# DMA loads tied to TensorE's progress, x tiles first, other DMA constants in the planner's model, and attention-weight normalisation in four parts, in a one-core kernel for linear attention and a gated MLP

## The chip, the cores and the metric

The kernel runs on one core of a Trainium2 chip. The metric is the device time of one execution, in microseconds (us). Lower is better. A profile shows a single execution; its span is some 1.8 us shorter than the device time of the same execution, and executions of one kernel on one chip differ, so times are compared by runs and gaps by profiles.

## The reference

Layernorm of x, then two branches on it: a linear-attention branch (32 heads of 32) and a gated MLP. The output is x + s * silu(mlp).

```python
x = A_x                                   # [1, 2048, 1024] bf16
xn = layernorm(x)
qkv = xn @ wqkv                           # heads: 32 of 32
pq, pk = phi(q), phi(k)                   # phi(t) = (t+1 if t>0 else exp(t)) + 1e-6
kv  = pk^T v ; z = sum_s pk               # per head
s   = ((pq kv) / (pq z + 1e-6)) @ wo
b   = (silu(xn @ w_gate) * (xn @ w_up)) @ w_down      # hidden size 3584
out = x + s * silu(b)
```

## The kernel before

The kernel is not written engine by engine. It calls helpers that record operations (engine, what is read and written, a planned duration). A *planner* then runs a small model of the engines over the recorded operations and fixes the static order of the instructions on TensorE (PE), VectorE (DVE), ScalarE (ACT), GpSimd and the DMA queue of SyncE (SP). Each engine executes its list in that order, waiting on semaphores. So the planner's durations decide no wait, but they decide what stands *behind* a wait.

```python
class Plan:
    def schedule(self):
        for o in reversed(ops):                       # latest start, from TensorE's cumulated work
            d = o.pecum if o.eng == "pe" else o.pecum + 30.0
            for s in o.succs:
                extra = (2.5 + o.nbytes / 250e3) if o.sem is not None else o.busy + o.lat
                d = min(d, s.dl - extra)
            o.dl = d - o.urgent
        # ... list scheduling: each engine takes, of what is ready, the earliest deadline;
        # ... TensorE takes the first ready of the next 6 operations in program order
            if o.sem is not None:                     # a DMA: one queue, in order
                free[e] = s + 0.08
                b = max(s + 0.7, dma_free)
                dma_free = b + o.nbytes / 300e3
                o.done = dma_free + 1.4
```

A DMA with no operand to wait for goes out as soon as its buffer is free. The attention weights are normalised in one piece per half of the rows (`p`): the reciprocals of the denominators are stored to DRAM, and 16 broadcasts bring them back; ACT scales each tile and DVE multiplies.

```python
def x_load(i):
    s = x_ring.take()                                 # 4 slots
    dma([], [s.r], s.ap(), xf[i*128:(i+1)*128, :], dsem(...), 256 * KB)

def normalise(p):                                     # called once per p, after weight pair 1
    for j in range(2):
        for hl in range(4):
            for q in range(2):
                dma([rscr], [rbr], rb[32*hl:32*hl+32, :, q, :], rows[:, q, :].partition_broadcast(32), ...)
        for g in range(8):
            act([z_r, zrr], [zrr], zr, zr, ACT.Identity, "sb", scale=zc[:, g:g + 1])
            tt([sr, zrr], [sr], dst, src, zr, ALU.mult, True)
    # ... four stores of 512 KB to q_scratch, read back for the last stage

def m_load(c):                                        # last stage: one buffer (MR) for four blocks c
    raw = W.at(MR, 4 * KB, FP16)...
    dma([mscr], [rr], raw, m_v[:, :, c*256:(c+1)*256], dsem("mld"), 512 * KB)
```

Order of the work: layernorm, transposes and k, v for 16 tiles (to 136 us); q, gate and up in weight pairs, first half of the rows (to 367); down-projection and combined attention weights `m` in four column blocks (to 467); the same two stages for the second half.

## Time and profile before

Three runs: 786.19, 787.03 and 787.52 us, median 787.03.

The busy line of the page, and the first line of the chain of work that ended last. In all profile lines PEld is TensorE's load of weights, SPq the sequencer of the DMA queue, `L195` a line of kernel.py; "..." marks lines left out.

```profile
PE 763.0 (97%) x3818; PEld 347.7 (44%) x3818; DVE 513.2 (65%) x945; ACT 305.0 (39%) x507; POOL 11.5 (1%) x33
...
PE 81%; DMA 10%; ACT 4%; DVE 3%; SPq 2%; issue 1%; ACTq 0%
```

TensorE is busy 763 of 787.9 us. Its 128x512 products last 379 ns each and start every 216 ns in a steady stretch. The Trainium skill ("TensorE: Matmul & The Clock Gate", Single matmul latency and Back-to-back issue gap) gives the formulas for these two numbers, (398 + N)/2.4 and N/2.4 + 2.5 ns, and the trace agrees with both. The page gives the second for an isolated product and about 131 ns for a real stream of weight loads and products at N = 512; this trace, which is such a stream, shows 216. A consequence for reading: an "idle before" of a product is what is left after the previous product's 379 ns, so the delay is about 0.16 us longer than that column says.

Since only TensorE's gaps can be won, they are read one by one. TensorE's timeline of before near the normalisation (start, length, what, in brackets the idle time before and who ended it):

```profile
196.75 17.44 PE L195 MATMUL ps<-X,W 128*128 128x512 f16 x80
215.74 3.63 PE L195 MATMUL ps<-X,W 128*128 128x512 f16 x16 [1.55 <-ACT ps L308]
219.96 6.28 PE L195 MATMUL ps<-X,W 128*128 128x512 f16 x28 [0.59 <-DVE ps L315]
227.25 13.12 PE L195 MATMUL ps<-X,W 128*128 128x512 f16 x60 [1.02 <-ACT ps L308]
```

That is 3.2 us of idle TensorE. The same view near 41 us, where a layernorm tile is late:

```profile
41.33 0.62 PE L202 MATMUL ps<-ident,W 128*128 128x128 f16 x8 [1.32 <-DVE veps L449]
...
43.07 1.90 PE L195 MATMUL ps<-H,X 128*128 128x512 bf16 x8 [0.65 <-ACT X L308]
```

And the DMA queue's timeline (start, time the queue's sequencer spent, what) for the time before that:

```profile
14.70 2.97 SPq L318 DMA_DIRECT2D W<-in_B_w_gate_dram  x1
17.71 1.72 SPq L318 DMA_DIRECT2D W<-in_B_w_up_dram  x1
19.47 4.78 SPq L318 DMA_DIRECT2D H<-in_A_wo_dram  x2
24.29 4.90 SPq L318 DMA_DIRECT2D W<-in_A_wqkv_dram  x2
29.23 30.57 SPq L318 DMA_DIRECT2D W<-in_A_x_dram  x10
```

x tile 4 is issued at 29.2, behind weights that are first needed after 136 us. In the last stage DVE is the one that stands. Its timeline, and then TensorE's:

```profile
382.96 0.69 DVE L315 TENSOR_TENSOR TM<-ps,TM 128x512 f32<-128x512 f32 x1 [1.67 <-PE ps L195]
391.31 2.98 DVE L315 TENSOR_TENSOR W<-W 128x896 f16<-128x896 bf16 x6 [7.67 <-DMA W<-in_B_w_down_dram]
394.21 0.69 DVE L315 TENSOR_TENSOR ps<-ps,TM 128x512 f32<-128x512 f32 x1
```

```profile
394.96 1.69 PE L195 MATMUL ps<-H,W 128*128 128x512 f16 x7 [1.25 <-DVE ps L315]
```

DVE waits 7.67 us for a down-projection weight block, then combines weights for 3 us, and only then does the addition in PSUM (394.21) that TensorE needs. Only two of the six combinations are of that block, from 391.31 to 392.6; the other four are of the `m` block, and wait for its reload. The chain that ended last runs through that reload (start, length, what):

```profile
386.19 6.53 DMA W<-m_scratch
392.74 1.11 DVE W L315 x3
...
394.21 0.70 DVE ps L315
```

Without these four the addition could have come some 1.6 us earlier (an estimate, 394.21 less 392.59), more than the gap of 1.25. The view of who waited for whom (total us, times, longest; in the same view ACT waits twice for broadcasts, at most 2.9 us):

```profile
DVE W L315 <- DMA W<-in_B_w_down_dram: 34.3, 8, 7.7
```

### The profile page before, as it was taken

The numbers are of one execution on the slowest core, as the hardware profiler recorded it, in microseconds if no ns is written. First come the engines' busy times: TensorE is split into PE (matmuls) and PEld (weight loads), VectorE is DVE, ScalarE is ACT, GpSimd is POOL, SyncE is SP. The second block draws the span as 40 slices with busy tenths as digits, with TensorE's granted clock in tenths as the row PEclk, the third lists the DMA queues.
The fourth block names the chain that finished last, engine by engine and source line by source line (L and its number), as shares of the span: only waits on it lengthen the run. The fifth ranks groups of instructions, "written<-read, shape, count | busy, mean of one in ns | idle before, by whom it ended". The sixth has DMA issues, their size and how long they took to land.

```text
span 787.9 us, 9684 instructions
## 1 busy us (share of the span) xinstructions
PE 763.0 (97%) x3818; PEld 347.7 (44%) x3818; DVE 513.2 (65%) x945; ACT 305.0 (39%) x507; POOL 11.5 (1%) x33
## 2 busy tenths in 40 slices
PE   8999999999999999999999999999999999999997
PEld 3445555444434444444444444344444444444443
DVE  5587432768597766886365676788776768557353
ACT  3344443555573334322222245547333332232131
POOL 2020000000000000000000000000000000000000
PEclk9999999999999999999999999999999999999999
DMA  9921000232883233370633623279423242251510
GB/s 310 277 67 41 1 1 1 81 107 63 190 246 106 73 89 106 94 222 9 197 92 82 183 71 96 66 156 296 143 63 106 76 126 62 59 171 50 154 41 27
DMA packets 142893, 86.74 MB, mean 110 GB/s; under 512 B 3328, under 2 KB 138752, under 8 KB 142848
## 3 DMA queue, kind: packets, MB, share of 16 engines
q1 hardware_dynamic: 142848, 86.13, 38.8%
q8 instruction: 30, 0.49, 0.3%
q14 instruction: 15, 0.12, 0.1%
HBM read 75.50 MB, written 10.62 MB: 109 GB/s over the span
## 4 chain that ended last, share of the span: by engine, by line
PE 81%; DMA 10%; ACT 4%; DVE 3%; SPq 2%; issue 1%; ACTq 0%
PE ps L195 79%; DMA W<-m_scratch 4%; ACT H L308 2%; PE ps L202 2%; SPq L318 2%; DMA H<-in_A_wqkv_dram 1%; DMA W<-in_B_w_down_dram 1%; DMA H<-r_scratch 1%; DVE W L315 1%; DMA W<-in_B_w_up_dram 1%; ACT TM L308 1%; DVE ps L315 1%; DMA m_scratch<-H 0%; DVE TM L315 0%; ACT ps L308 0%
## 5 line engine op out<-in xcount | busy, mean ns | idle before, releaser
L195 PE MATMUL ps<-X,W 128*128 128x512 f16 x1504 | 346.7, 379 | 7.7 <-DVE TM L315 2.8
L308 ACT ACTIVATE TM<-ps 128x512 f32<-128x512 f32 (+2 forms) x300 | 177.0, 596 | 302.6 <-PE ps L195 302.2
L195 PEld LDWEIGHTS ps<-X,W 128*128 128x128 f16 (+1 forms) x1504 | 143.4, 98 | 184.5 <-DVE ps L315 5.7
L315 DVE TENSOR_TENSOR W<-W 128x1024 f16<-128x1024 bf16 (+3 forms) x224 | 137.3, 629 | 73.2 <-DMA W<-in_B_w_down_dram 34.3
L195 PE MATMUL ps<-H,W 128*128 128x512 f16 x672 | 153.3, 379 | 4.2 <-DVE ps L315 4.0
L195 PE MATMUL ps<-P,W 128*128 128x512 f16 x512 | 122.9, 379 | 1.5 <-ACT ps L308 1.5
L195 PEld LDWEIGHTS ps<-H,W 128*128 128x128 f16 (+1 forms) x672 | 64.7, 98 | 82.2 <-DVE ps L315 7.1
L315 DVE TENSOR_TENSOR ps<-ps,TM 128x512 f32<-128x512 f32 x80 | 55.6, 695 | 69.5 <-PE ps L195 69.5
L315 DVE TENSOR_TENSOR TM<-ps,TM 128x512 f32<-128x512 f32 (+1 forms) x112 | 68.2, 610 | 36.5 <-PE ps L195 27.0
L308 ACT ACTIVATE ps<-ps 128x512 f32<-128x512 f32 x80 | 47.0, 587 | 101.2 <-PE ps L195 101.0
L195 PEld LDWEIGHTS ps<-P,W 128*128 128x128 f16 (+1 forms) x512 | 49.2, 98 | 60.8 <-ACT ps L308 2.0
L315 DVE TENSOR_TENSOR H<-ps,TM 128x512 f16<-128x512 f32 x84 | 57.4, 685 | 4.7 <-PE ps L195 3.3
L195 PE MATMUL ps<-H,X 128*128 128x512 bf16 x256 | 57.3, 379 | 2.6 <-ACT X L308 1.8
L195 PE MATMUL ps<-H,P 128*128 128x512 bf16 x256 | 56.6, 379 | 0.0
L308 ACT ACTIVATE TM<-TM 128x512 f16<-128x512 f32 (+1 forms) x54 | 33.5, 620 | 56.6 <-DVE TM L315 56.4
L315 DVE TENSOR_TENSOR H<-H 128x1024 f16<-128x1024 f16 (+1 forms) x74 | 41.6, 571 | 12.2 <-ACT H L308 11.2
L494 DVE TENSOR_SCALAR TM<-TM 128x512 f16<-128x512 f16 x64 | 17.9, 290 | 41.6 <-ACT TM L308 41.1
L195 PEld LDWEIGHTS ps<-H,X 128*128 128x128 f16 x256 | 24.4, 98 | 31.0 <-ACT X L308 2.1
L195 PEld LDWEIGHTS ps<-H,P 128*128 128x128 f16 x256 | 24.7, 98 | 28.3
L315 DVE TENSOR_TENSOR W<-H 128x1024 f16<-128x1024 f16 x38 | 25.4, 685 | 0.5
L308 ACT ACTIVATE H<-H,zc 128x512 bf16<-128x512 bf16 x32 | 20.8, 716 | 5.0 <-DMA H<-r_scratch 5.0
L495 DVE SCALAR_TENSOR_TENSOR W<-ps,TM 128x512 bf16<-128x512 f32 x32 | 22.0, 688 | 0.8
(60 smaller groups left out, 307.9 us busy)
## 6 DMA issues: line engine op xcount, KB each, us to landing
W<-in_B_w_gate_dram SPq DMA_DIRECT2D x28, 512.0 KB, 3.9
W<-in_B_w_up_dram SPq DMA_DIRECT2D x28, 512.0 KB, 5.2
W<-in_B_w_down_dram SPq DMA_DIRECT2D x16, 896.0 KB, 7.1
W<-in_A_x_dram SPq DMA_DIRECT2D x16, 256.0 KB, 4.1
H<-in_A_wqkv_dram SPq DMA_DIRECT2D x4, 1024.0 KB, 8.8
W<-in_A_wqkv_dram SPq DMA_DIRECT2D x8, 512.0 KB, 7.5
TM<-in_A_x_dram SPq DMA_DIRECT2D x16, 256.0 KB, 4.2
H<-r_scratch SPq DMA_DIRECT2D x32, 128.0 KB, 4.2
```

Source lines behind the costliest of these rows:

```text
L195: last = h.matmul(o, l, r, start=st, stop=sp, skip_group_check=True)
L202: last = h.transpose(o, i, ident)
L308: return PL.op("act", reads, writes, lambda h: h.activation(o, i, func, **kw), nel(o) / 1200.0 + (0.055 if src == "ps" else 0.095))
L315: return dve(reads, writes, lambda h: h.tensor_tensor(o, a, b, op), nel(o), 1.92 if fast else 0.96)
L318: return PL.op("sp", reads, writes, lambda h: h.dma_start(o, i), 0.08, sem=s, nbytes=nbytes, cow=cow)
L494: dve([e.r], [b.r], lambda h: h.tensor_scalar(ba, ea, 1.0, EPS_PHI, ALU.min, ALU.add), 512, 2.6)
L495: dve([src_r, b.r], [out_r], lambda h: h.scalar_tensor_tensor(out_ap, src, 0.0, ba, ALU.max, ALU.add), 512)
```

## The change

The intent: (1) every load gets an extra predecessor, the TensorE operation that the plan places 12 us before the load's latest start, so that loads stop running far ahead of need; x tiles get 10 us of priority; the deadline allowance of a DMA grows. (2) The planner's model of a DMA becomes slower. (3) The normalisation is cut into four parts, spread over weight pairs 2 and 3, its broadcasts held to a TensorE product.

```diff
-                extra = (2.5 + o.nbytes / 250e3) if o.sem is not None else o.busy + o.lat
+                extra = (4.0 + o.nbytes / 200e3) if o.sem is not None else o.busy + o.lat
...
+        pes = [o for o in ops if o.eng == "pe"]
+        cum = [o.pecum + o.busy for o in pes]
+        for o in ops:
+            if o.sem is not None and o.succs:
+                k = bisect_right(cum, o.dl - self.lead) - 1          # lead = 12.0
+                if k >= 0 and pes[k] not in o.preds:
+                    o.preds.add(pes[k])
+                    pes[k].succs.append(o)
...
-                b = max(s + 0.7, dma_free)
-                dma_free = b + o.nbytes / 300e3
-                o.done = dma_free + 1.4
+                b = max(s + 1.0, dma_free)
+                dma_free = b + o.nbytes / 230e3
+                o.done = dma_free + 1.8
...
-            dma([], [s.r], s.ap(), xf[i * 128:(i + 1) * 128, :], dsem("x%d" % s.k), 256 * KB)
+            dma([], [s.r], s.ap(), xf[i * 128:(i + 1) * 128, :], dsem("x%d" % s.k), 256 * KB).urgent = 10.0
...
-        def normalise(p):
-            for j in range(2):       # 8 broadcasts, then 8 scalings and products; twice
+        def normalise_part(p, j, half):   # 4 broadcasts (after=PL.lastpe), 4 scalings and products, 1 store
...
+                    if 2 <= n <= 3:
+                        at = tuple((4 + 6 * h, partial(normalise_part, p, n - 2, h)) for h in range(2))
-                    normalise(p)
```

The denominators' scratch also gets another layout, so that a broadcast reads runs of 1 KB in place of 512 bytes.

More of the change, by code (lines that the diff above doesn't have):

```diff
@@ L1 @@
+from bisect import bisect_right
 from collections import deque
@@ L35, with __init__ @@
     LAT = {"pe": 0.22, "act": 0.2, "dve": 0.2, "pool": 0.2}
-    def __init__(self, window):
+    def __init__(self, window, lead):
         self.ops = []
@@ L42, in __init__, with op @@
         self.window = window
-    def op(self, eng, reads, writes, fn, busy, sem=None, nbytes=0, urgent=0.0, cow=None):
+        self.lead = lead
+    def op(self, eng, reads, writes, fn, busy, sem=None, nbytes=0, urgent=0.0, cow=None, after=None):
         o = Op()
@@ L55, in op @@
             preds.update(cow.preds)
+        if after is not None:
+            preds.add(after)
         for r in writes:
@@ L77, in op @@
             self.pecum += busy
+            self.lastpe = o
         self.ops.append(o)
@@ L203, in _tr_group, with build_kernel @@
     return last
-def build_kernel(nc, A_x, A_wqkv, A_wo, B_w_gate, B_w_up, B_w_down, out, WINDOW=6, NWARM=14):
+def build_kernel(nc, A_x, A_wqkv, A_wo, B_w_gate, B_w_up, B_w_down, out, WINDOW=6, NWARM=14, LEAD=12.0):
     S, D, FF = 2048, 1024, 3584
@@ L264, in build_kernel @@
         q_scr = nc.dram_tensor("q_scratch", [2, 2, 2, 128, 4 * 512], FP16)
-        r_scr = nc.dram_tensor("r_scratch", [2, 4, 32, 256], BF16)
+        r_scr = nc.dram_tensor("r_scratch", [2, 2, 32, 512], BF16)
         ps = [es.enter_context(nc.psum_tensor("ps%d" % b, [128, 512], F32)) for b in range(8)]
@@ L287, in dsem @@
             return semn[name]
-        PL = Plan(WINDOW)
+        PL = Plan(WINDOW, LEAD)
         MM = 0.2137
@@ L315, in tt, with dma @@
             return dve(reads, writes, lambda h: h.tensor_tensor(o, a, b, op), nel(o), 1.92 if fast else 0.96)
-        def dma(reads, writes, o, i, s, nbytes, cow=None):
-            return PL.op("sp", reads, writes, lambda h: h.dma_start(o, i), 0.08, sem=s, nbytes=nbytes, cow=cow)
+        def dma(reads, writes, o, i, s, nbytes, cow=None, after=None):
+            return PL.op("sp", reads, writes, lambda h: h.dma_start(o, i), 0.08, sem=s, nbytes=nbytes, cow=cow,
+                         after=after)
         class Ring:
@@ L774, in recip @@
             act([rr], [er], rb, ra, ACT.Identity, "sb")
-            dma([er], [named("rscr", p)], r_scr[p].rearrange("q h t -> (q h) t"), rb, dsem("rs"), 64 * KB)
-        RB0 = 68 * KB
-        def normalise(p):
-            for j in range(2):
-                rb = H.at(RB0 + j * 8 * KB, 8 * KB).rearrange("p (g q t) -> p g q t", g=NG, q=2)
-                rbr = H.reg(RB0 + j * 8 * KB, 8 * KB)
-                first = None
-                for hl in range(4):
-                    rows = r_scr[p, 2 * j:2 * j + 2, :, :].rearrange("q (g h) t -> h g q t", h=4)[hl]
-                    for q in range(2):
-                        o0 = dma([named("rscr", p)], [rbr], rb[32 * hl:32 * hl + 32, :, q, :],
-                                 rows[:, q, :].partition_broadcast(32), dsem("rr%d_%d_%d" % (j, hl, q)), 128 * KB, first)
-                        first = first or o0
-                for g in range(NG):
-                    src, sr = pq_tile(g, j)
-                    dst = src.bitcast(FP16)
-                    o = RB0 + j * 8 * KB + g * KB
-                    zr, zrr = H.at(o, KB), H.reg(o, KB)
-                    act([z_r, zrr], [zrr], zr, zr, ACT.Identity, "sb", scale=zc[:, g:g + 1])
-                    tt([sr, zrr], [sr], dst, src, zr, ALU.mult, True)
-            for j in range(2):
-                for k in range(2):
-                    o = PQ0 + (2 * k + j) * 4 * KB
-                    dma([H.reg(o, 4 * KB)], [named("q", p, k, j)], q_scr[p, k, j], H.at(o, 4 * KB, FP16),
-                        dsem("pq%d%d" % (k, j)), 512 * KB)
@@ new lines, in recip @@
+            o0 = None
+            for q in range(4):
+                t0 = (q % 2) * 256
+                o1 = dma([er], [named("rscr", p)], r_scr[p, q // 2, :, t0:t0 + 256], rb[32 * q:32 * q + 32, :],
+                         dsem("rs%d" % q), 16 * KB, o0)
+                o0 = o0 or o1
+        RB0 = 68 * KB
+        def normalise_part(p, j, half):
+            o = RB0 + (2 * j + half) * 4 * KB
+            rb, rbr = H.at(o, 4 * KB).rearrange("p (g t) -> p g t", t=512), H.reg(o, 4 * KB)
+            first = None
+            for hl in range(4):
+                rows = r_scr[p, j].rearrange("(g h) t -> h g t", h=4)[hl, 4 * half:4 * half + 4]
+                o0 = dma([named("rscr", p)], [rbr], rb[32 * hl:32 * hl + 32, :, :], rows.partition_broadcast(32),
+                         dsem("rr%d_%d_%d" % (j, half, hl)), 128 * KB, first, PL.lastpe)
+                first = first or o0
+            for gl in range(4):
+                g = 4 * half + gl
+                src, sr = pq_tile(g, j)
+                dst = src.bitcast(FP16)
+                zr, zrr = H.at(o + gl * KB, KB), H.reg(o + gl * KB, KB)
+                act([z_r, zrr], [zrr], zr, zr, ACT.Identity, "sb", scale=zc[:, g:g + 1])
+                tt([sr, zrr], [sr], dst, src, zr, ALU.mult, True)
+            o = PQ0 + (2 * half + j) * 4 * KB
+            dma([H.reg(o, 4 * KB)], [named("q", p, half, j)], q_scr[p, half, j], H.at(o, 4 * KB, FP16),
+                dsem("pq%d%d" % (half, j)), 512 * KB)
@@ L818, in gu_load, with gu_pair @@
             return wload([wg_v[:, :, n * 256:(n + 1) * 256], wu_v[:, :, n * 256:(n + 1) * 256]])
-        def gu_pair(p, n, stat):
+        def gu_pair(p, n, stat, at=()):
             sgs = {}
@@ L831, in ev_u @@
                 tt([r, s.r], [orr], o, ap, s.ap(FP16), ALU.mult)
-            run_pair(xset(stat, 0, XV[p], ev_g, d_ring), xset(stat, 1, XV[p], ev_u, d_ring))
+            run_pair(xset(stat, 0, XV[p], ev_g, d_ring), xset(stat, 1, XV[p], ev_u, d_ring), at)
             if n % 2 == 1:
@@ L1001, in build_kernel @@
                 else:
-                    gu_pair(p, n, st)
+                    at = ()
+                    if 2 <= n <= 3:
+                        at = tuple((4 + 6 * h, partial(normalise_part, p, n - 2, h)) for h in range(2))
+                    gu_pair(p, n, st, at)
                 pump(2)
```

## The prediction

> **What bounds it now.** TensorE. The page shows PE busy 763.0 of 787.9 us (97%), clock 1.00 in all stages. Steady matmuls follow each other every 0.215 us in the timeline; the change leaves their number alone. Only PE's idle time can be won: 24.9 us. Its parts in the PE timeline: start, 8.3-13.4: 1.9; 41.3-43.1: 2.0 (a layernorm tile); 140: 0.3; 174.9: 0.9; 215.7-227.3: 3.2 (ACT, DVE); 373-377: 1.1; 395: 1.3; 423: 0.3; 531.9: 1.5; 554.0: 1.1; 650.8: 1.7; 679: 1.4; 695-698: 0.8; 744: 1.2; end: 1.5.
>
> **What the change does, and the gap it meets.**
> 1. *x tiles first, weights held back.* The SP timeline shows x tile 4 issued only at 29.2, behind 5 MB of weights not needed before 136; it landed at 36.5. The Trainium skill ("DMA: Bandwidth & Descriptors", Queues, rings and completion order) says that each DMA engine consumes descriptors in ring order; this trace agrees: loads issued 10.7-29.2 landed in order of issue, 8.5-11 us later. With those held back, the 2.0 us at 41-43 goes. At the start two more x tiles come before the first weight load (about 0.85 us each at that window's 310 GB/s), but PE then has several tiles for each weight block: about 0, +1 at worst.
> 2. *Normalisation in quarters.* Now 16 broadcasts go out in one burst (0.45-0.5 us each on SP; landing 208.3-218.4), ACT sits in order behind them (2.9 us at 213.4), then mixes 16 scalings of 0.71 us with evictions PE waits for. Four parts, each with 4 broadcasts held to a PE product, half the descriptors, spread over two weight pairs: I expect 2.5 of 3.2 back near 215-227, 1.3 of 1.5 at 532, 1.0 of 1.1 at 554 (there the weight load took 8.7 us behind q stores and reloads; the reloads are now held back).
> 3. *A slower DMA in the planner's model* (230 GB/s, 1.8 us tail). It fixes the static order of DVE. Today DVE is ordered to combine a weight block that has not landed: it stood 7.7 us (382-391) and 2.3 (647-649.5) for down-projection weights, and PE's gaps at 395 and 650.8 follow. The old model gives a lone 896 KB load 5 us; the trace shows 5.9-9.8. The new one, 6.8 alone and 10.8 as second of a pair, fits. I expect 3.5 back of the 5.9 at 395, 423, 651, 679 and 744.
>
> Unchanged: 140, 175, 373 and 695 (one buffer for the combined weights), the end.
>
> **Added.** Only waits of the DMA queue. Each load still goes out some 18 us of PE work before its use, against 4-10 us to landing.
>
> **Sum.** 2.0 + 2.5 + 1.3 + 1.0 + 3.5 = 10.3 off; minus 1.8 for new short stalls, as every static order is redone: 8.5. **Predicted 778.5 us, 772.5 to 784.5.** Faster by over 2% (under 771.3) 0.07, within 2% 0.90, slower 0.03.
>
> **To see in the profile.** PE busy about 763, span near 779; no PE gap near 40; DMA rate low from 20 to 110 us, the first pairs' weights issued after 100; four groups of four broadcasts; no DVE wait above 3 us for down-projection weights; no weight load of 8 us near 545.
>
> **What would make it wrong.** Held loads bunching before the last stage (down weights, reloads, m) into a new DMA wait; ACT ordered to scale before a broadcast lands, in four places instead of one; a first weight block over 1 us later; DVE, 95% busy at 220-240, remaining the brake there.

## The result, and the profile after

Three runs: 774.91, 776.97 and 777.79 us, median 776.97, against 787.03 before. The ratio is 0.9868 (95% interval 0.9835 to 0.9902). Ratios here and below are the mean time of one kernel's runs over that of the other's runs of the same rounds, so they are not quite the ratio of the medians. In a later measurement of five rounds the changed kernel had a median of 776.51 us against 789.5, ratio 0.9849 (run e4 below). The two profiled executions, 789.71 (not one of the three runs above) and 774.91 us, happen to lie further apart than the medians.

The page of after:

```profile
PE 759.9 (98%) x3802; PEld 349.8 (45%) x3818; DVE 519.1 (67%) x945; ACT 306.2 (40%) x507; POOL 11.7 (2%) x33
...
PE 94%; ACT 2%; DVE 2%; DMA 1%; issue 0%; POOL 0%
```

The chain that ended last had 10% of its time on DMAs and now has 1%. (Of this trace 16 matmul records are missing; the work is the same.) TensorE's timeline near the normalisation is one unbroken row where before there were three gaps:

```profile
195.53 44.63 PE L209 MATMUL ps<-X,W 128*128 128x512 f16 x206
```

The DMA queue's timeline: x tiles no longer stand behind weights, and the first pairs' weights go out after 115 us.

```profile
10.22 79.12 SPq L332 DMA_DIRECT2D W<-in_A_x_dram  x12
115.94 1.00 SPq L332 DMA_DIRECT2D W<-in_A_wqkv_dram  x2
```

DVE's timeline in the last stage: the addition in PSUM at 387.08 now comes before the weight combination, and DVE's longest wait for that block is 1 us.

```profile
379.31 0.69 DVE L329 TENSOR_TENSOR TM<-ps,TM 128x512 f32<-128x512 f32 x1 [1.68 <-PE ps L209]
387.08 0.70 DVE L329 TENSOR_TENSOR ps<-ps,TM 128x512 f32<-128x512 f32 x1 [7.08 <-PE ps L209]
...
391.44 0.62 DVE L329 TENSOR_TENSOR W<-W 128x896 f16<-128x896 bf16 x1 [0.99 <-DMA W<-in_B_w_down_dram]
```

And the wait shown of before (ACT's longest wait for a broadcast is now 0.7 us):

```profile
DVE W L329 <- DMA W<-in_B_w_down_dram: 3.0, 3, 1.1
```

What got worse: the start. TensorE's idle before 15 us grew from 1.9 to 2.8 us in this profile (4.1 in that of e4). Layernorm of tile 1 is mixed into that of tile 0 here, and the transposes of tile 1 stand before the second product; but another order only moved the gaps (e10 below), so the cause is not shown.

### The profile page after: what moved, and what is told of

Its sections match the earlier page's. It is cut to its first block, busy times and chain, and to the rows that moved or that the text cites. A ratio compares the mean times of both kernels' runs of the same rounds, so it can differ in the third digit from the quotient of the medians. Undisturbed runs are those within 1.5% of the kernel's fastest.

```text
span 773.2 us, 9708 instructions
## 1 busy us (share of the span) xinstructions
PE 759.9 (98%) x3802; PEld 349.8 (45%) x3818; DVE 519.1 (67%) x945; ACT 306.2 (40%) x507; POOL 11.7 (2%) x33
## 4 chain that ended last, share of the span: by engine, by line
PE 94%; ACT 2%; DVE 2%; DMA 1%; issue 0%; POOL 0%
PE ps L209 92%; PE ps L216 2%; DMA W<-m_scratch 1%; ACT H L322 0%; DVE W L329 0%; ACT TM L322 0%; DMA W<-in_A_x_dram 0%; ACT L322 0%; DVE TM L329 0%; ACT X L322 0%; ACT ps L322 0%; DVE ps L329 0%; DVE stats L461 0%; DVE stats L462 0%; DVE H L600 0%
## 5 line engine op out<-in xcount | busy, mean ns | idle before, releaser
L329 DVE TENSOR_TENSOR W<-W 128x1024 f16<-128x1024 bf16 (+3 forms) x224 | 134.2, 628 | 10.8 <-PE ps L209 4.7
L209 PE MATMUL ps<-W 128*128 128x512 f16 x76 | 21.8, 379 | 0.0
```

The costliest lines, as they stand in the source:

```text
L209: last = h.matmul(o, l, r, start=st, stop=sp, skip_group_check=True)
L329: return dve(reads, writes, lambda h: h.tensor_tensor(o, a, b, op), nel(o), 1.92 if fast else 0.96)
```

## The experiments

The change has three parts that can be switched separately: **G** (gates, deadline allowance, x priority), **S** (the planner's DMA model) and **Q** (quarters). Theory M: S mends everything that depends on the static order, G only the late x tile, Q part of the normalisation. Rival G: the gates do it all, by keeping loads from crowding each other. Rival Q: quarters are what cures the normalisation. Twelve kernels ran; all gave correct results. Each was compared, in five rounds, with the kernel before on the same chip (its median there 788.7 to 789.6 us); e1 to e4, e5 to e8, e9 to e11 and e12 had a chip each, so runs of different groups are compared by their ratios. First the summary; the columns on the right are sums of TensorE's gaps of over 0.2 us in the profile of each run, by stretch (before: first profile and first measurement, while the ratios are to the kernel before on the run's own chip; the stretches move by a few us between kernels; "start" leaves out the first 1.4 us, and in before a gap of 0.15).

| run | parts | median us | ratio, 95% interval | start, to 30 | x tile, 41-45 | 214-230 | 365-377 | 393-425 | 530-555 | 640-682 | 683-698 | 705-745 |
|---|---|---|---|---|---|---|---|---|---|---|---|---|
| before | none | 787.0 | 1 | 1.8 | 2.0 | 3.2 | 1.1 | 1.5 | 2.6 | 3.1 | 0.6 | 1.2 |
| e1 | S | 779.38 | 0.9879 (0.9852-0.9907) | 3.3 | 2.9 | 0.8 | 0.6 | 0 | 0.8 | 0 | 1.1 | 0 |
| e2 | G | 784.30 | 0.9941 (0.9920-0.9962) | 4.6 | 0 | 2.7 | 1.3 | 0 | 2.5 | 0 | 0.7 | 0 |
| e3 | Q | 786.94 | 0.9975 (0.9949-1.0001) | 1.8 | 2.2 | 2.1 | 0.6 | 1.8 | 1.9 | 1.3 | 0.6 | 1.2 |
| e5 | S Q | 778.13 | 0.9849 (0.9826-0.9873) | 2.6 | 2.3 | 0 | 1.0 | 0 | 0 | 0 | 0.6 | 0 |
| e6 | G Q | 781.31 | 0.9891 (0.9870-0.9913) | 2.1 | 0 | 2.0 | 1.6 | 0 | 2.0 | 0 | 1.8 | 0.2 |
| e7 | G S | 784.24 | 0.9938 (0.9914-0.9962) | 2.3 | 0 | 2.4 | 1.8 | 0 | 2.9 | 0 | 0.7 | 0 |
| e4 | G S Q | 776.51 | 0.9849 (0.9823-0.9875) | 4.1 | 0 | 0 | 2.4 | 0 | 0 | 0 | 0.7 | 0 |

### e1, e2, e3: each part alone, and e4, all together

Edits: the kernel before with only the DMA model lines (e1), only the gate, allowance and priority lines (e2), only the quarters (e3); e4 is the changed kernel.

```diff
# e1, all that acts (the record's diff also carries unused parameters)
-                b = max(s + 0.7, dma_free)
-                dma_free = b + o.nbytes / 300e3
-                o.done = dma_free + 1.4
+                b = max(s + 1.0, dma_free)
+                dma_free = b + o.nbytes / 230e3
+                o.done = dma_free + 1.8
```

> The kernel before with one line group changed: the planner simulates a DMA as 1.0 us + bytes at 230 GB/s + 1.8 us (was 0.7, 300 GB/s, 1.4). No load is held, the normalisation is whole. Theory M (the model corrects the static order of DVE and ACT): the TensorE gaps of the last stages at 395, 423, 651, 679 and 744 (5.9 us together) mostly go, no DVE wait above 3 us for down-projection weights, the gap at 41-43 stays: about 782, 4 to 6 us faster. Rival G (the gates do it, by keeping loads from crowding each other): under 1.5 us faster, the gaps at 395 and 651 stay.

> The kernel before with the gates alone: every load held to a TensorE product, x tiles first, larger allowance in the deadlines; old DMA model, whole normalisation. Theory M: the gap at 41-43 (2.0 us) goes, perhaps that at 554 (1.1), up to 1 us is lost at the start; the gaps at 395, 651, 679, 744 and 215-227 stay: about 784.5, 1 to 4 us faster. Rival G: 6 us or more faster, with the gaps of the last stages gone.

> The kernel before with the normalisation in four parts alone (its broadcasts held to a TensorE product, nothing else held), old DMA model. Theory M: the gaps at 215-227 (3.2 us) and 532 (1.5) shrink to under 1.5 together, that at 41-43 and those of the last stages stay: about 783, 3 to 5 us faster. Rival G: with the old model and ungated loads the broadcasts still land late, ACT stands in four places: under 2 us faster.

> The changed kernel once more, on the same chip as the three parts: 775 to 778 if the first measurement holds. If the parts act on separate gaps, the three single gains add up to about this gain; if they need each other, their sum is clearly smaller.

Measured: 1.2% faster by the model alone, more than expected; 0.6% by the gates alone; 0.25% by the quarters alone, with an interval that touches no change (theory M had expected 3 to 5 us of them: a miss). The three gains add to 2.05% and the whole gave 1.51%, so they overlap. Three numbers in the planner gave most of the gain, and they also cleared most of the *normalisation's* gaps, which the prediction had put down to the quarters; what the numbers changed in the order there was not read. Rival G is half right: the gates alone also cleared 393-425, 640-682 and 705-745, as I had said they would not. With quarters alone, the normalisation's gaps only fell from 3.2 to 2.1 and from 2.6 to 1.9.

What was wrong with the old model is told by one comparison. The planner's own reckoning is a by-product of the program, so its time for each DMA can be set beside the time that the trace shows from issue to landing, and its length for the whole program beside the span. Means, in us:

```
                              down-projection block   m reload        whole program
                              planned   trace         planned trace   planned   span
before                        5.70      7.01          3.98    5.14    769.8     787.9
S alone (e1)                  7.99      6.88          6.39    4.60    784.9     776.6
after                         7.72      6.44          6.95    5.10    772.1     773.2
```

Before, the planner was optimistic by 1.2 to 1.3 us for these loads. It placed the combination of a block where it believed the block had landed, ahead of additions that TensorE waits for (six of them at 391.31 above). Its plan was 18 us shorter than the span. With a pessimistic model the plan is longer (in e1 by 15 us, of which a wait of 10.8 for the x tile near 54, where the trace of e1 shows 2.9) and the execution shorter. The DVE wait itself is not the harm. In e1 DVE still waits for these blocks, five times and up to 6.0 us, and the addition in PSUM is still ordered behind the wait, yet TensorE has no gap there. DVE's timeline of e1:

```profile
380.46 0.69 DVE L321 TENSOR_TENSOR TM<-ps,TM 128x512 f32<-128x512 f32 x1 [1.68 <-PE ps L201]
385.59 1.28 DVE L321 TENSOR_TENSOR W<-W 128x896 f16<-128x896 bf16 x2 [4.44 <-DMA W<-in_B_w_down_dram]
389.74 0.70 DVE L321 TENSOR_TENSOR ps<-ps,TM 128x512 f32<-128x512 f32 x1 [2.86 <-PE ps L201]
```

Two combinations stand before the addition in place of six (those of the `m` block now come after it, from 390.9 on), and it is the addition that waits, 2.86 us, for TensorE. The block also lands earlier, 5.1 us after the start of the operation at 380.46, against 8.3 us after the same operation at 382.96 in before: the model sets the order of the DMA queue too, and in e1 one load of x goes out ahead of the block, in before two. Which of the two changes of order did more was not tested.

The x tile is another matter. It is late because weights are in front of it, and the new constants leave them there; e1's TensorE timeline keeps the gap:

```profile
42.71 0.62 PE L208 MATMUL ps<-ident,W 128*128 128x128 f16 x8 [2.04 <-DVE veps L456]
...
44.67 1.67 PE L201 MATMUL ps<-H,X 128*128 128x512 bf16 x7 [0.87 <-ACT X L314]
```

### e5, e6, e7: all but one part, and e8, all but the x priority

Edits: the changed kernel without the gates, allowance and priority (e5), with the old DMA model (e6), with `normalise` whole (e7), without `.urgent = 10.0` (e8).

> DMA model and quarters, no load held, x tiles not first. The model alone left gaps of 2.9 us near 42-45 (x tile), 0.8 near 225 and 0.8 near 539. Theory M (the model mends all that depends on static order, the gates only the x tile): the gap near 42 stays at 2 to 3 us, those at 225 and 539 shrink, last stages clean: ratio to before about 0.987, some 2 us slower than the whole change. Rival G: the last stages get gaps back, ratio above 0.991.

> Gates, x tiles first and quarters, with the old DMA model in the planner. Gates alone had already cleared the gaps at 395, 651 and 744, but not those near 219-227 (2.7) and 536-544 (2.5). Theory M: those near 215-230 and 535-545 stay at over 1.5 us each, quarters or not, since ACT is still ordered too early; ratio 0.990 to 0.995. Rival Q (quarters cure the normalisation once loads are held): both stretches under 0.5 us, ratio 0.985 to 0.987 like the whole change.

> Gates, x tiles first and the DMA model, with the normalisation whole. Theory M: the model alone had brought the normalisation's gaps from 3.2 to 0.8 and from 1.5 to 0.8, so at most 1.5 us slower than the whole change: ratio 0.985 to 0.987. Rival Q: gaps of 2 us or more return at 215-227, ratio 0.989 or above.

> The whole change without the 10 us of priority for x tiles. If x tiles first costs time at the start (two x tiles ahead of the first weight block, and layernorm of tile 1 mixed in before tile 0 is done), TensorE's gaps before 15 us shrink from 2.8-4.1 to about 1.8 and nothing comes back at 41-43, because holding the weights is what lets x tile 4 through: 1 to 2 us faster than the whole change, ratio about 0.983. If the priority is what lets the x tiles through, a gap of 2 us returns near 41-43 and the ratio rises to 0.988.

Measured: e5 0.9849, as fast as the whole within the intervals, where theory M had expected some 2 us slower; the gap near 42 stays, as it said, but the start is shorter (2.6 us, against 4.1 in e4). So once the model and the quarters are in, the gates, with the priority and the allowance, add nothing that these runs can resolve. e6 0.9891: the normalisation's stretches keep 2.0 us each, quarters or not, as theory M said. e7 0.9938: a miss for theory M, as rival Q had it. Gates and model together, with the burst, are slower than the model without gates (0.9879). e8 0.9839 (0.9815 to 0.9862, median 777.19), again not distinguishable from the whole. The x tiles get through without priority (no gap near 42), so holding the weights is what lets them through; but the start did not get shorter: gaps of 1.12 at 8.8 and 2.89 at 15.3 and two small ones, 4.5 us in all. So the priority is worth nothing that these runs can resolve.

In e7 a gap also slows what follows it. TensorE's timeline, and then the windows view (stretch, length, busy time and count of PE, PEld, DVE, ACT and POOL, granted clock, DMA share, GB/s):

```profile
229.06 7.30 PE L209 MATMUL ps<-X,W 128*128 128x512 f16 x26 [2.35 <-DVE ps L329]
```

```profile
226.00:229.00 3.00, 0.71 (x4) 0.10 (x2) 2.62 (x7) 3.00 (x7) 0.00 (x0) 0.96 0.94 281
229.00:232.00 3.00, 2.94 (x7) 1.04 (x8) 2.81 (x6) 0.58 (x2) 0.00 (x0) 0.50 1.18 325
232.00:236.00 4.00, 4.00 (x20) 1.83 (x19) 2.90 (x6) 1.71 (x3) 0.00 (x0) 0.98 0.29 115
```

After the gap the granted clock is 0.50: 7 products in 3 us, where 4 us at nearly the full clock hold 20. The clock record of this trace gives 3.41 us at 0.5 from 228.8. TensorE worked in the last 3.1 us of them; half of that, 1.5 us, is an estimate of the extra loss. The same happened once in e3 (from 215.4, after a gap of 2.13) and in e5 (from 42.8, after 2.04). The Trainium skill ("TensorE: Matmul & The Clock Gate", Part 1) says that the array runs at half rate after at least one idle window of about 3.4 us and that the window is free-running. The half rate and a stretch of 3.4 us are what the trace shows; the gaps here were shorter than the window. The clock records of e3, e5 and e7 lie on such a grid: the fall comes 61.0, 11.0 and 65.0 times 3.413 us after the first record at full clock. Added up over each window of that grid, TensorE idled 2.13, 2.04 and 2.04 us in the three that ended with the fall. The longer gaps of e9 (2.47 and 2.52) and e8 (2.89) were each split between two windows, at most 1.85 us in one, and brought no fall. The border is not sharp: one window of e2 with 2.04 us and one of e1 with 1.98 us brought none either. This is read from the traces (each execution's end left out), not tested. The six runs of e7 had mean clocks of 0.994 to 0.996, so this is a steady part of its loss.

### e9: the burst, with the true cost of a scaling

In e7, 16 scalings run in a burst; back to back they take 0.61 us each and the planner reckons 0.522. In that trace ACT falls behind its plan from 1.9 us to 3.35 us during the burst. e9 is e7 with that cost corrected.

```diff
-                         nel(o) / 1200.0 + (0.055 if src == "ps" else 0.095))
+                         nel(o) / 1200.0 + (0.19 if "scale" in kw else 0.055 if src == "ps" else 0.095))
```

> All but quarters (whole normalisation, which measured 0.9938), with one number of the planner changed: a scaling of attention weights on ACT is reckoned at 0.617 us instead of 0.522; back to back it takes 0.61 in the traces (four in 2.55 us, eight in 5.00). If the burst hurts because 16 scalings each run 0.09 us over plan, so that the evictions ordered among them come late, the gaps of 2.4 us near 229 and 2.6 near 548 shrink below 1 us each and the ratio falls to 0.987 or less. If it hurts because the broadcasts land late or crowd the weight loads, the gaps stay and the ratio stays at 0.992 or above.

Measured: 784.33 us, ratio 0.9944 (0.9924 to 0.9965). The profile is of the fastest of the six runs (780.58; the others took 783.2 to 786.0, at mean clocks of 0.994 to 0.997 where it had 0.999). The gaps stayed:

```profile
229.22 7.08 PE L209 MATMUL ps<-X,W 128*128 128x512 f16 x32 [2.47 <-DVE ps L329]
```

This idea of mine fell, and cleanly. With the corrected cost ACT's distance to its plan stays at 1.92 to 1.98 us over the burst, so the planner now foresees the burst rightly, and the gap is still there, because it is *in the plan*: the planner itself reckons TensorE idle 2.98 us near 227 and 3.02 near 542. A correct plan of a bad sequence does not help.

### e12: the burst, with an earlier release of the loads

Two DMA queue timelines explain why the plan has that gap. e7:

```profile
200.77 0.38 SPq L332 DMA_DIRECT2D W<-in_B_w_gate_dram  x1
201.20 0.58 SPq L332 DMA_DIRECT2D W<-in_B_w_up_dram  x1
203.36 0.34 SPq L332 DMA_DIRECT2D r_scratch<-TM  x1
...
207.74 7.72 SPq L332 DMA_DIRECT2D H<-r_scratch  x16
```

The gate releases a weight load at 200.8; the denominators' store, issued at 203.4, takes 4.3 us beside it; the 16 broadcasts start at 207.7 and occupy the queue for 7.7 us; the next weights go out at 216.9 and the second of them lands at 224.4 (212.7 and 220.5 in e12). e12 is e7 with one number changed, and so has the burst still.

```diff
-def build_kernel(..., WINDOW=6, NWARM=14, LEAD=12.0):
+def build_kernel(..., WINDOW=6, NWARM=14, LEAD=18.0):
```

> All but quarters (0.9938), with the lead of the gates 18 us instead of 12. In that run the weight load for the second pair, held until 200.8, is in flight when the attention denominators are stored (that store takes 4.3 us instead of 2.3), the 16 broadcasts start 3 us later, and the next weight load, queued behind them, lands at 224.4; TensorE idles 2.4 near 229 and 2.6 near 548. If the gates' late weight loads colliding with the burst are the cause, loads released 6 us earlier are out of its way: both gaps under 0.5 us and ratio 0.984 to 0.987, as with quarters. If the burst alone is the cause, the gaps stay and the ratio is 0.992 or above.

Measured: 777.74 us, ratio 0.9854 (0.9824 to 0.9883), all six runs with a mean clock of 0.999 or 1.0. The queue of e12, and then TensorE:

```profile
194.76 0.44 SPq L332 DMA_DIRECT2D W<-in_B_w_gate_dram  x1
...
199.57 0.32 SPq L332 DMA_DIRECT2D r_scratch<-TM  x1
...
203.49 7.86 SPq L332 DMA_DIRECT2D H<-r_scratch  x16
```

```profile
222.15 14.19 PE L209 MATMUL ps<-X,W 128*128 128x512 f16 x64 [0.34 <-ACT ps L322]
```

The store now takes 2.1 us, the burst starts 4.2 us earlier, the gap near 222 is 0.34 and that near 538 is 0.8 us (over the 0.5 forecast). The planner's own reckoning of e12 has no gap near 227 or 542. So gates and burst collide: a load released 12 us ahead meets the burst, one released 18 us ahead is out of its way. The one number moves every gate, so that this load's release is the cause is read from the queue and the plan, not isolated. Quarters with a lead of 12 and a whole normalisation with a lead of 18 measure the same (0.9849 and 0.9854). Quarters are one cure of a clash that the gates make; without gates (e1 against e5) they are worth 0.3%, which the intervals do not separate from nothing.

### e10 and e11: towards a faster version

e10 is the changed kernel with the first eight loads in a fixed order and TensorE's first 14 operations after the warm-up in program order. e11 adds another order in the second column block of the last stage, which begins with D1, a product that does not need the late `m` block.

```diff
+        XU = {0: 200.0, 1: 180.0, 2: 150.0, 3: 130.0}      # e10: urgency of x0..x3
+        WU = {0: 190.0, 1: 170.0, 2: 160.0, 3: 140.0}      # and of the four kv weight blocks
...
-                        if n >= self.window:
+                        if n >= (1 if len(done) < 28 else self.window):
+            if c == 1:                                       # e11 only
+                seq = "D1 S1 S5 S2 S6 S7 S3 D5 S4 D6 D2 D7 D3 D4"
```

> The whole change, with the first eight loads put in the order x0, first kv weights, x1, second, third, x2, fourth, x3, and TensorE held to program order for its first 14 operations. In the kernel as changed layernorm of tile 1 is mixed into that of tile 0 and the transpose of tile 1 stands behind the first product; TensorE idles 2.8 to 4.1 us before 13. If that order is the cause: first product at about 8.3 instead of 9.3-9.5, gaps before 20 down to about 1.5, 1.5 to 2.5 us faster than the whole change, ratio about 0.982. If the loads' rate is the limit: same gaps, ratio 0.985.

> As the run before, and the second column block of the last stage begins with product D1, which needs no combined weights, in place of S1. The load into their single buffer is issued at 367 and lands at 372 (681 and 685 in the second half). If the gaps near 369-373 and 683 (1.2 to 2.4 and 0.7 to 0.8 us) are that buffer's wait and the turn before it, they go: 1.5 to 2.5 us faster than the run before, ratio about 0.980. If the gap is only pushed to the next block, no change.

Measured: e10 775.34 us, ratio 0.9835 (0.9819 to 0.9851), which overlaps with that of the changed kernel: inconclusive. The first product did come earlier (8.5), but the gaps only moved: in e11, which starts alike, they are 1.12 us at 8.9, 1.47 at 12.3 and 1.12 at 20.9.

My expectation of 1.5 us of gaps at the start was wrong: now the transposes wait for layernorm of tiles 1 and 2, and e10's profile has 4.1 us of gaps there in all. What limits the start stays open.

e11: 773.56 us, ratio 0.9809 (0.9793 to 0.9825). TensorE's timeline after the change, where the second column block begins, and then that of e11:

```profile
369.13 0.40 PE L216 MATMUL ps<-ident,TM 128*128 128x128 f16 x4 [0.74 <-DVE TM L329]
369.36 1.67 PE L209 MATMUL ps<-H,W 128*128 128x512 f16 x7
370.87 0.39 PE L216 MATMUL ps<-ident,TM 128*128 128x128 f16 x4
371.76 1.04 PE L209 MATMUL ps<-X,W 128*128 128x512 f16 x4 [0.50 <-DMA W<-m_scratch]
```

```profile
369.45 1.67 PE L209 MATMUL ps<-H,W 128*128 128x512 f16 x7
370.96 0.39 PE L216 MATMUL ps<-ident,TM 128*128 128x128 f16 x4
371.19 1.67 PE L209 MATMUL ps<-H,W 128*128 128x512 f16 x7
372.70 0.39 PE L216 MATMUL ps<-ident,TM 128*128 128x128 f16 x4
372.92 3.35 PE L209 MATMUL ps<-X,W 128*128 128x512 f16 x14
```

Both gaps are gone (e10's profile has the first alone), and so is that at 683; none came back in a later block. 1.8 us between the medians of e10 and e11 on the same chip agree with the gaps removed (0.74 near 370 and 0.74 near 683 in e10's profile, plus 0.16 for each; that profile also has 0.36 near 541, which e11's lacks). e11 is the fastest version that ran, 1.9% faster than the kernel before.

## Why the prediction was right

The total was right: 778.5 us predicted, within 772.5 to 784.5, and 776.97 measured, with "within 2%" given 0.90. Its account of where the time lies, TensorE's gaps one by one, held. Its account of which edit mends which gap did not hold everywhere, and so the total says little for it: some 13.5 us of gaps went where 10.3 were forecast, the gain was 10.1 us (7.7 to 13.0 by the interval of the ratio) where 8.5 was forecast, and e5 has the same gain without the gates, to which the first 2.0 us of the sum belong.

- *The x tile, 2.0 us, from the held weights:* right. The gap is gone in every run with gates and there in every run without (e1, e3, e5). What it misses: in e5 the gap also cost 3.4 us at half clock. (One figure of it is off: x tile 4 landed 7.3 us after its issue, not 8.5 to 11; the order of landing is as it says.)
- *The start, "about 0, +1 at worst":* at the edge in the first profile of after, which shows 0.9 us more idle than before, and too low for that of e4, 2.2.
- *Normalisation, 2.5 of 3.2, 1.3 of 1.5 and 1.0 of 1.1:* the size was a little low, since all three gaps went; the cause was half of it. Quarters alone (e3) left 2.1 and 1.9 us. The DMA model alone (e1) left 0.8 and 0.8. Both together (e5) left none. In the whole change both are needed: without the quarters 2.4 and 2.9 us come back (e7), without the model 2.0 and 2.0 (e6).
- *Last stages, 3.5 of 5.9, from the model:* undersized. All of it went. That the model alone does it is shown by e1, which changes nothing else; how it does (the combinations of the `m` block behind the addition, or an earlier down-projection block) is read from the trace only. The prediction named the wait for down-projection weights alone; at 395, 423 and 744 the wait that ended last was that for the reload of `m` (4 combinations behind it, 1.0 us of waiting at 421.3 and at 742.2). It is not the only cure: the gates alone cleared the same gaps (e2), which the prediction did not see. Why they did was only looked at, not tested: in that trace the same addition in PSUM is ordered before the weight combination. So it is in the trace of the whole change (387.08 before 391.44), while in e1 it stays behind.
- *"Added: only waits of the DMA queue":* this failed, though the full change hides it. The gates' lead of 12 us collides with the burst of broadcasts (e7 against e12), and it costs 0.6% where the normalisation is whole (e7 against e1). In the full change the quarters pay for that.
- *Minus 1.8 us for new short stalls:* of the right size. New or longer in the profile after: 0.9 at the start, 0.4 near 140, 0.2 near 370, 0.25 at 462.
- *What to see:* span 773.2 where 779 was stated; no gap near 40, first pairs' weights at 115.9, four groups of four broadcasts, DVE's longest wait for down-projection weights 1.1 us, weight loads near 545 of 4.6 and 5.7 us. All of these as stated.

## What to carry to other kernels

In this kernel with statically ordered engines, a planner that was optimistic about DMA was worse than one that was pessimistic: the early guess put more work ahead of the additions that TensorE needs. Compare planned with traced durations before changing the program's structure; here three constants gave 1.2% and the structural parts less by themselves, 0.6% and 0.25%. A load that is held back must be released early enough to pass the largest burst on its queue (here 18 us ahead, not 12), and parts of a change have to be tried with and without each other, since two that cure the same gap do not add, and two that collide subtract.

## What the Trainium skill lacked or had wrong

- "TensorE: Matmul & The Clock Gate", Part 1 and HAM oscillation: the page ties the fall to half rate to an idle window, or gap, of about 3.4 us. Here it fell to 0.50 for 3.41 us after gaps of only 2.04, 2.13 and 2.35 us (e5, e3, e7), but not in the profiles with gaps of 2.04 (e1), 2.47 and 2.52 (e9) and 2.89 (e8). So gaps of about 2 us can already trigger it, and length alone does not tell: in the three cases 2.04 to 2.13 us of idle lay in one window of 3.41 us, in e9 and e8 at most 1.85.
- "DMA: Bandwidth & Descriptors", Issuing engines are not separate DMA queues: it calls the sequencer's time to start a DMA usually small relative to the DMA. That holds for each broadcast of 128 KB, 0.48 to 0.49 us against 4.3 to 4.4 us on average from issue to landing (e7, e12). What the page lacks is that it adds up: 16 of them kept the queue's sequencer for 7.7 to 7.9 us.
- The same page, Anatomy of one DMA: it fits a fixed cost, about 2.0 us, for the GpSimd path alone, and none from issue to landing for the SyncE path. Here seven of the eight stores of 16 KB to DRAM on the SyncE path took 1.40 to 1.49 us from issue to landing.
- No page that I read treats the choice of DMA constants for a static planner. Here 0.7 us + 300 GB/s + 1.4 us was too optimistic for the loads that mattered (5.70 planned, 7.01 traced), and 1.0 us + 230 GB/s + 1.8 us was safely pessimistic (7.72 and 6.44).
